# A feed-forward stage run in two halves of its inner width, with partial sums kept in DRAM

## The chip, the cores and the metric

The kernel runs on one core of one Trainium2 chip. The metric is the device time of one execution in microseconds (us). A core has five engines that work through their own queues in order: TensorE (PE, matrix products; PEld is its weight load), VectorE (DVE), ScalarE (ACT), GpSimd (POOL) and SyncE (SP, which here only starts transfers). Results of products go to PSUM, everything else lives in SBUF, and transfers to and from DRAM are started from the queues of SP, ACT and POOL.

## The reference

Three layers follow one another: a gated recurrent attention (4 x 8 heads, 768 steps, head size 40), a mixture of 8 experts of which each token takes one, and a plain feed-forward layer. Only the last is touched by the change:

```python
def _moe_ref(x, w_gate, w1, w2):            # x: 3072 tokens x 320
    ...
    out[mask] = gate_w[mask, None] * (np.maximum(xe @ w1[e], 0.0) @ w2[e])

def _moe2_ref(x, w_in, w_out):              # w_in: 320 x 2048, w_out: 2048 x 320
    h = x @ w_in
    g = np.maximum(0.01 * h, h)
    return (g @ w_out).astype(np.float32)
```

The expert's gate weight is one factor per token, and the leaky maximum is homogeneous for positive factors, so the kernel multiplies by it at the very end.

## The kernel before

Every product is made of three: each factor is split into a high part (rounded by ACT) and a low part (the rest, subtracted by DVE or GpSimd), and high x high, low x high and high x low are summed in PSUM.

After the attention, the expert stage runs over eight experts, each with a fixed share of up to 512 tokens. Expert e computes eight first-layer sums (`expert_up`, 8 inner pieces f) and then three groups of second-layer sums (`expert_down`, a = 0, 1, 2), which are copied into `x2T`, the transposed input of the feed-forward, 3072 tokens and 512 spare columns wide. For a = 2 ACT copies half of the rows (L1409) and DVE adds the other half (L1410). During expert 7's three groups `ffn_x` also splits the first 512 tokens of the feed-forward (`xf`).

The feed-forward `ffn` runs over six windows of 512 tokens and, within each, over 16 inner pieces f of 128 columns: loop index i = 0 to 95. For each i TensorE does eight products of 512 columns (`up`, L217, quarter f // 4 of `w_in`), ACT scales by 0.01 (L1540), DVE takes the maximum (L1541), ACT rounds the high part (L1544) and DVE subtracts the low part (L1546). Three pieces later (LAG) come twelve products of 320 columns (`down`, L1506 to L1508), which add into four PSUM accumulators `po`, one for each 128 tokens. They live in four banks, so the next window's sums can begin only when the last window's are evicted. At f = 15 they are evicted with the gate factor, two by DVE (L1517), two by ACT (L1515), and scattered to their rows of the result by POOL (`put_rows`, L93). The first three inner pieces' products with the first two thirds of x are issued ahead, because the last third comes late.

The feed-forward's weights come as 8-byte numbers and are converted on the chip while the experts and the feed-forward run. There are 20 pieces: `("i", quarter, a)`, 12 of them, and `("o", f2, 0)`, eight output pieces of two f each. A piece takes five steps (`piece_step`), step n belonging to piece n // 5: step 0 stores the piece before (two transfers on ACT's queue, each behind the part that it stores) and takes exponent and mantissa apart (DVE, L1247 and L1248); step 1 is one ACT operation (L1250); step 2 two on DVE (L1255, L1256); step 3 one on DVE (L1260) and ACT's rounding (L1275); step 4 two on GpSimd (L1280, L1281), and the raw load of a later piece. Scratch tiles `d_e`, `d_a`, `d_s` exist once.

`run_side` does the next step. In the experts it is called at the places listed in `SIDE` (numbers 0 to 7 are the first-layer pieces, 8 to 13 the two halves of each second-layer group), in the feed-forward after L1544 (k = 0) and after L1546 (k = 1) of each inner piece. Before the feed-forward 66 steps are done (expert 7's last group holds steps 64 and 65); it does the other 35 at 2.25 per inner piece.

The tiles of three input quarters are there all along; the fourth quarter's can be had only when the experts' hidden tiles (`hh`, `hl`) are free, so its pieces (the stored ones) are converted into scratch, written to DRAM (`wi_d`) and loaded by POOL's queue at the start of the feed-forward (L1337). The output weights lie in tiles that the experts' weights leave free (`wo_tiles`). All converted output pieces, and the fourth input quarter, are also kept in DRAM for a closing loop over tokens beyond the experts' shares, which runs zero times here.

Of the kernel before, what the change touches and what calls it, by code (L numbers as in the profile page):

```python
# [51 lines left out]
def tile_mlstm_moe_ffn(  # L52
# [24 lines left out]
    xs_d = dp.tile([E * NT, DM], F32, tag="xs_d", name="xs_d")  # L77
    list_d = dp.tile([NT, 2], I32, tag="list_d", name="list_d")
    wi_d = dp.tile([2, 3, P, CAP], F32, tag="wi_d", name="wi_d")
    wo_d = dp.tile([2, NF, P, DM], F32, tag="wo_d", name="wo_d")  # L80
    g_d = dp.tile([BH, S], F32, tag="g_d", name="g_d")

# [1141 lines left out]
    def stored(q):  # L1224

        kind, i, j = pieces[q]
        return kind == "i" and i >= NQ - 1

    def piece_step(n):
        q, t = divmod(n, 5)  # L1230
        if t == 0 and q > 0:
            piece_store(pieces[q - 1])
        if q >= len(pieces):
            return
        p = pieces[q]
        kind, i, j = p
        n = CAP if kind == "i" else 2 * DM
        raw = st["raw", p]
        coded = raw.dtype != F32

        def tmp(tg, dt=I32):
            return mp.tile([P, 2 * DM], dt, tag=tg, name=f"{tg}{kind}{i}_{j}")[:, 0:n]

        if t == 0 and coded:
            h = raw[:, :, 1]
            ex, man = st["ex"], st["man"] = tmp("d_e"), tmp("d_a")
            nc.vector.tensor_scalar(ex, h, 20, 0x7FF, ALU.logical_shift_right, ALU.bitwise_and)  # L1247
            nc.vector.tensor_scalar(man, h, 12, 9, ALU.logical_shift_left, ALU.logical_shift_right)  # L1248
        if t == 1 and coded:
            nc.scalar.activation(st["ex"], st["ex"], AF.Relu, bias=bexp, scale=2.0**23)  # L1250
        if t == 2 and q > 0 and stored(q - 1) and q + 1 < len(pieces):
            piece_load(pieces[q + 1])
        if t == 2 and coded:
            sc = st["sc"] = tmp("d_s")
            nc.vector.scalar_tensor_tensor(sc, raw[:, :, 1], -(2**31), st["ex"], ALU.bitwise_and, ALU.bitwise_or)  # L1255
            nc.vector.tensor_tensor(st["man"], st["man"], sc, ALU.bitwise_or)  # L1256
        if t == 3:
            if coded:
                w = raw[:, :, 0].bitcast(U32)
                nc.vector.scalar_tensor_tensor(st["ex"].bitcast(F32), w, 2.0**-52, st["sc"].bitcast(F32), ALU.mult, ALU.mult)  # L1260
            val = st["val"] = st["man"].bitcast(F32) if coded else raw
            if kind == "i" and i < NQ - 1:
                st["hl"] = [(wiq[i][0][j], wiq[i][1][j], slice(0, n))]
                st["out", p] = None
            elif kind == "o":
                cut = [(0, 2)] if wo_at(2 * i)[2] == wo_at(2 * i + 1)[2] else [(0, 1), (1, 2)]
                st["hl"] = st["out", p] = [
                    (wo_at(2 * i + a)[0][:, 0 : (b - a) * DM], wo_at(2 * i + a)[1][:, 0 : (b - a) * DM], slice(a * DM, b * DM)) for a, b in cut
                ]
            else:  # L1270

                lo = raw.rearrange("p n t -> p (n t)")[:, 0:n].bitcast(F32R) if coded else tmp("d_s", F32R)
                st["hl"] = st["out", p] = [(tmp("d_h", F32R), lo, slice(0, n))]
            for hi, _, sl in st["hl"]:
                nc.scalar.copy(hi, val[:, sl])  # L1275
        if t == 4:
            for hi, lo, sl in st["hl"]:
                val = st["val"][:, sl]
                if coded:
                    nc.gpsimd.tensor_tensor(val, val, hi.bitcast(F32), ALU.subtract)  # L1280
                    nc.gpsimd.tensor_tensor(lo, val, st["ex"].bitcast(F32)[:, sl], ALU.add)  # L1281
                else:
                    nc.gpsimd.tensor_tensor(lo, val, hi.bitcast(F32), ALU.subtract)
            st.pop(("raw", p))
            if q + 2 < len(pieces) and not stored(q):
                piece_load(pieces[q + 2])
# [13 lines left out]
    wo_t = {}  # L1300

    def wo_tiles(nm, part):
        if part == 0:
# [10 lines left out]
        i, r = (0, f) if f < 8 else (1, f - 8) if f < 14 else (0, 8) if f == 14 else (2, 0)  # L1314
        return wo_t[i, 0][:, r * DM :], wo_t[i, 1][:, r * DM :], (i, f == 14)

    pieces = [("i", qd, a) for qd in range(NQ) for a in range(3)] + [("o", f2, 0) for f2 in range(NF // 2)]
    side_at = [0]

    def run_side(end=5 * len(pieces)):  # L1320
# [4 lines left out]
    def load_wo(f0, f1):  # L1325
        for hl in range(2):
            nc.gpsimd.dma_start(
                wo_at(f0)[hl][:, 0 : (f1 - f0) * DM].rearrange("p (a d) -> p a d", d=DM), wo_d[hl, f0:f1].rearrange("a p d -> p a d")
            )

    def load_wi(nm):
        ih = [t[0] for t in wiq]
        il = [t[1] for t in wiq]
        for hl, (dl, tg) in enumerate(((ih, "hh"), (il, "hl"))):
            ts = [mp.tile([P, CAP], F32R, tag=tg, name=f"wi{nm}{tg}{a}", bufs=8) for a in range(3)]
            for a in range(3):
                nc.gpsimd.dma_start(ts[a], wi_d[hl, a])  # L1337
            dl.append(ts)
        return ih, il

    def tiles_fx(nm, odd=0):
        return tiles_x(f"f{nm}", "xr", "raw") if odd else tiles_x(f"f{nm}")
# [83 lines left out]
    for i in range(24):  # L1426
        extras.setdefault((2 + i // 4, 2 * (i % 4) + 1), []).append(lambda i=i: list_rows(i, i + 1))
    SA = 5, 6, 7, 8, 9, 11, 13
    SB = 0, 1, 4, 6, 7, 9, 11, 13
    SC = 0, 1, 4, 6, 7, 9, 11, 13  # L1430
    SD = 0, 1, 4, 6, 7, 9, 11, 13
    SE_ = 0, 1, 4, 6, 7, 9, 11, 13
    SF = 0, 1, 4, 6, 7, 9, 11, 13
    SG = 0, 1, 4, 6, 7, 9, 11, 13
    SH = 0, 1, 4, 6, 7, 8, 9, 10, 11, 12, 13

    SIDE = (SA, SB, SC, SD, SE_, SF, SG, SH)

# [4 lines left out]
    for e in range(E):  # L1443
# [11 lines left out]
        if not last:  # L1455
            e_r = nc.sync.value_load(slots[0:1, 0, e + 1 : e + 2], min_val=0, max_val=E - 1)
            row = nc.sync.value_load(slots[0:1, 1, e + 1 : e + 2], min_val=0, max_val=(E - 1) * NT)
            xr = x_rows_tile(e + 1)
            x_load(xr, row, 0, CAPS[e + 1])
            w1raw = load_w1(of_expert(w1, e_r), e + 1)  # L1460
            w1n = tiles_w1(e + 1)
            xs = tiles_x(e + 1)
        else:
            xf = tiles_fx("a0")
            assert side_at[0] <= 5 * 3 * NQ + 3
            wo_tiles("a", 0)
        w2u = w2s

        def in_down(a, k, e=e, last=last):
# [17 lines left out]
            w1s = w1n  # L1487
            w2raw, w2s = load_w2(of_expert(w2, e_r), e + 1), tiles_w2(e + 1)

    def ffn(nm, wins, wi, metas, x0, side=lambda i, k: None, W=CAP):  # L1490
        wih, wil = wi
        nw = len(wins)
        xs = {0: x0}
        gs, pos = {}, {}
        LAG = 3

        def down(fs, w):
            if fs[0] == 0:
                pos[w] = [pm.tile([P, DM], F32, tag="dn" if n < 2 else "tr", name=f"po{nm}{w}_{n}") for n in range(W // P)]
            po = pos[w]  # L1500
            gw = [gs.pop(w * NF + f) for f in fs]
            for n in range(W // P):
                tsl = slice(n * P, (n + 1) * P)
                for f, (g_h, g_l) in zip(fs, gw):
                    woh, wol = (t[:, 0:DM] for t in wo_at(f)[0:2])
                    nc.tensor.matmul(po[n], g_h[:, tsl], woh, start=(f == 0), stop=False)  # L1506
                    nc.tensor.matmul(po[n], g_h[:, tsl], wol, start=False, stop=False)  # L1507
                    nc.tensor.matmul(po[n], g_l[:, tsl], woh, start=False, stop=(f == NF - 1))  # L1508
                if fs[-1] < NF - 1:
                    continue  # L1510
                mt = metas(w, n)
                ot = mp.tile([P, DM], F32, tag=("d_e", "d_s", "d_a", "d_h")[n], name=f"ot{nm}{w}_{n}")
                gate = mt[:, 1:2].bitcast(F32)
                if n % 2:
                    nc.scalar.activation(ot, po[n], AF.Copy, scale=gate)  # L1515
                else:
                    nc.vector.tensor_scalar(ot, po[n], gate, None, ALU.mult)  # L1517
                put_rows(out_w, (), out, mt[:, 0:1], ot)

        FIRST = 4  # L1520
        pus = {}

        def up(i, part):
            w, f = divmod(i, NF)
# [3 lines left out]
            up_mms(pus[i], xs[w], wih[f // 4], wil[f // 4], fs, part)  # L1528

        for i in range(FIRST - 1):  # L1530
            up(i, slice(0, 6))
        for i in range(nw * NF + LAG):
            if i < nw * NF:
                w, f = divmod(i, NF)
# [11 lines left out]
                nc.vector.tensor_tensor(g_l, lk, g_h.bitcast(F32), ALU.subtract)  # L1546
                side(i, 1)
                gs[i] = g_h, g_l
                if f == 10 and w + 1 < nw:
                    xs[w + 1] = ffn_x(tiles_fx(f"{nm}{w + 1}", (w + 1) % 2), wins[w + 1])  # L1550
            if i >= LAG:
                w, f = divmod(i - LAG, NF)
                if w + 1 < nw or f < NF - 4:
                    down([f], w)
                elif f == NF - 3:
                    down([NF - 4], w)
                elif f == NF - 1:
                    down([NF - 3, NF - 2, NF - 1], w)
# [12 lines left out]


    n_win = nc.values_load(tab[0:1, 0, 0:1], min_val=0, max_val=MW)
# [75 lines left out]
```

## Time and profile before

| | us |
|---|---|
| median of 3 timed runs | 779.99 |
| lowest and highest | 776.85, 780.35 |
| the profiled execution, whole | 781.25 |
| its span | 779.5 |
| its TensorE busy | 733.8 (94%) |
| its DVE busy | 469.3 (60%) |
| its ACT busy | 364.5 (47%) |
| its GpSimd busy | 256.5 (33%) |

The profile is of one execution. The span is the time from its first to its last instruction; the whole time has 1.75 us around it. Rows of it are shown below in groups: a row of the timeline has start and duration in us, then engine, line of the kernel, operation, output <- inputs, sizes; in square brackets the idle time of the engine just before and what ended it. A busy time of TensorE is modelled, so stretches in which it is busy throughout but at half its clock also count as busy; the granted clock stands beside it.

### The profile page before, as it was taken

How to read it: one execution, taken by the hardware profiler on the slowest of the kernel's cores; microseconds unless marked ns; L12 is line 12 of the kernel's file. 1: busy time of each engine (PE TensorE's matmuls, PEld its weight loads, DVE VectorE, ACT ScalarE, POOL GpSimd, SP SyncE). 2: the span in 40 equal slices, each digit the busy share in tenths (PEclk: the TensorE clock that was granted, in tenths of full speed). 3: DMA queues.
4: the chain of work that ended last, by engine and by line, in shares of the span. 5: the costliest groups of instructions: out<-in, count | busy, mean ns of one | idle time of the engine just before them, and what ended most of it. 6: DMA issues, size and time to landing. Idle time of an engine off the chain costs nothing.

```text
span 779.5 us, 12185 instructions
## 1 busy us (share of the span) xinstructions
PE 733.8 (94%) x4226; PEld 646.7 (83%) x4226; DVE 469.3 (60%) x1023; ACT 364.5 (47%) x799; POOL 256.5 (33%) x414
## 2 busy tenths in 40 slices
PE   8998999988989999999899979999999999999992
PEld 4786877877868899999897768999999999998992
DVE  6576777875687766778576776544344344344330
ACT  4675765523445545656444444343333343343330
POOL 7645667517133344246444333101002002002002
PEclk7998999987999999999999999999999999999996
DMA  6899566233635656765867421000000000000001
GB/s 165 253 321 298 162 179 198 92 99 111 187 111 179 166 131 175 165 150 143 228 131 235 144 90 60 26 1 18 18 1 26 9 1 34 1 1 34 1 1 37
DMA packets 58320, 85.31 MB, mean 109 GB/s; under 512 B 9423, under 2 KB 38895, under 8 KB 58255
## 3 DMA queue, kind: packets, MB, share of 16 engines
q1 hardware_dynamic: 44975, 56.67, 26.4%
q10 hardware_dynamic: 9344, 18.35, 7.5%
q0 software_dynamic: 3936, 9.47, 3.6%
q8 instruction: 35, 0.57, 0.3%
q14 instruction: 30, 0.25, 0.1%
HBM read 64.42 MB, written 19.95 MB: 108 GB/s over the span
## 4 chain that ended last, share of the span: by engine, by line
issue 35%; PE 19%; DVE 7%; POOL 6%; DMA 5%; ACT 3%; ACTq 0%; POOLq 0%; SPq 0%; DVEq 0%
PE pu L217 9%; PE pd L1403 8%; POOL out_dram L93 3%; DMA w1r<-in_moe_w_dram 3%; POOL d_ao L1280 1%; PE pt L243 1%; DVE lka L1541 1%; POOL woaw1l L1281 1%; DVE d_ao L1256 1%; DVE d_so L1255 1%; ACT d_eo L1250 1%; PE pva L217 1%; DVE w1l L164 1%; DMA rdo<-in_moe_w_out_dram 1%; DVE hl L248 1%
## 5 line engine op out<-in xcount | busy, mean ns | idle before, releaser
L217 PE MATMUL pva<-xhfa,wi 128*128 128x512 f32 x432 | 134.2, 393 | 0.0
L1541 DVE TENSOR_TENSOR lka<-pva,lka 128x512 f32<-128x512 f32 x96 | 66.3, 691 | 108.2 <-ACT lka L1540 106.3
L1540 ACT ACTIVATE lka<-pva 128x512 f32<-128x512 f32 x96 | 57.2, 596 | 120.1 <-PE pva L217 110.2
L93 POOL DMA_INDIRECT out_dram<-ota,meta x24 | 24.0, 999 | 263.8 <-DVE ota L1517 259.7
L1546 DVE TENSOR_TENSOR gla<-lka,gha 128x512 fp32r<-128x512 f32 x96 | 67.9, 707 | 59.0 <-ACT gha L1544 58.3
L1544 ACT CAST gha<-lka 128x512 fp32r<-128x512 f32 x96 | 59.6, 621 | 84.2 <-DVE lka L1541 81.2
L217 PEld LDWEIGHTS pva<-xhfa,wi 128*128 128x128 f32 x432 | 78.4, 188 | 12.7 <-DVE xhfa L198 0.2
L1508 PE MATMUL poa<-woaw1h,gla 128*128 128x320 f32 x216 | 67.1, 310 | 2.0 <-DVE gla L1546 2.0
L546 ACT ACTIVATE E<-pD,wn 128x128 f32<-128x128 f32 x192 | 56.1, 366 | 25.5 <-PE pD L543 19.7
L217 PE MATMUL pu<-xh,w1h 128*128 128x256 f32 (+7 forms) x192 | 65.8, 344 | 1.8 <-DVE xh L198 1.7
L1506 PE MATMUL poa<-woaw1h,gha 128*128 128x320 f32 x216 | 66.7, 309 | 0.7 <-ACT ota L1515 0.7
L1507 PE MATMUL poa<-woaw1l,gha 128*128 128x320 f32 x216 | 66.8, 309 | 0.1
L217 PE MATMUL pu<-xh,w1l 128*128 128x256 f32 (+7 forms) x192 | 65.2, 341 | 0.0
L589 PEld LDWEIGHTS pI<-nv,P 128*128 128x128 f32 x384 | 54.2, 202 | 10.3 <-DVE P L557 4.7
L589 PE MATMUL pI<-nv,P 128*128 128x123 f32 (+1 forms) x384 | 56.6, 284 | 3.4 <-DVE P L557 3.4
L217 PE MATMUL pva<-xlfa,wi 128*128 128x512 f32 x144 | 56.0, 389 | 0.0
L555 PE MATMUL pS<-qB,nK 120*128 120x384 f32 (+1 forms) x132 | 54.9, 498 | 0.0
L1507 PE MATMUL poa<-woaw2l,gha 128*128 128x320 f32 x144 | 45.9, 319 | 5.1 <-POOL woaw2l L1281 5.1
L1403 PE MATMUL pd<-hh,w2h 128*128 128x512 f32 (+6 forms) x128 | 46.0, 359 | 0.0
L1508 PE MATMUL poa<-woaw2h,gla 128*128 128x320 f32 x144 | 45.8, 318 | 0.1
L1506 PE MATMUL poa<-woaw2h,gha 128*128 128x320 f32 x144 | 45.5, 316 | 0.4 <-ACT gha L1544 0.2
L1403 PE MATMUL pd<-hl,w2h 128*128 128x512 f32 (+6 forms) x128 | 45.6, 356 | 0.2 <-DVE hl L248 0.2
(302 smaller groups left out, 1825.6 us busy)
## 6 DMA issues: line engine op xcount, KB each, us to landing
w2r<-in_moe_w_dram SPq DMA_DIRECT2D x16, 640.0 KB
w1r<-in_moe_w_dram SPq DMA_DIRECT2D x16, 512.0 KB
xs_d<-zr SPq DMA_DIRECT2D x16, 320.0 KB
rdo<-in_moe_w_out_dram ACTq DMA_DIRECT2D x16, 320.0 KB
w1r<-in_moe_w_dram SPq DMA_DIRECT2D x32, 128.0 KB
rdi<-in_moe_w_in_dram ACTq DMA_DIRECT2D x8, 512.0 KB
no<-in_o_gate_dram SPq DMA_DIRECT2D x12, 320.0 KB
nv<-in_v_dram SPq DMA_DIRECT2D x10, 328.0 KB
```

Of the source, the lines that this page charges most:

```text
L217: nc.tensor.matmul(ps_t, a, b, start=start, stop=stop)
L546: nc.scalar.activation(Et[:, j], pD[:, j], AF.Exp, bias=wn[:, c, 3, HG * g + j : HG * g + j + 1])
L555: nc.tensor.matmul(pS[:, :nh], nats["K", c][:R, g], QB[p][:R, g - GCUT[p], :nh], start=True, stop=True)
L589: nc.tensor.matmul(pI[:, r0:, j], Pt[:, j], vj, start=True, stop=True)
L1403: nc.tensor.matmul(pd, aa, bb, start=(i == 0), stop=(i == len(seq) - 1))
L1506: nc.tensor.matmul(po[n], g_h[:, tsl], woh, start=(f == 0), stop=False)
L1507: nc.tensor.matmul(po[n], g_h[:, tsl], wol, start=False, stop=False)
L1508: nc.tensor.matmul(po[n], g_l[:, tsl], woh, start=False, stop=(f == NF - 1))
L1540: nc.scalar.activation(lk, pu, AF.Copy, scale=0.01)
L1541: nc.vector.tensor_tensor(lk, pu, lk, ALU.max)
L1544: nc.scalar.copy(g_h, lk)
L1546: nc.vector.tensor_tensor(g_l, lk, g_h.bitcast(F32), ALU.subtract)
```

## The change

The feed-forward's loop order becomes: half h of the inner width (8 of the 16 inner pieces), and within it all six windows. Each of the 12 units (h, w) has its own sums, and each window's tokens are split into high and low parts twice. At the end of a unit of the first half the four accumulators are evicted with the gate factor (two by DVE, two by ACT as before), three of them into the spare columns of `x2T`, and stored to DRAM (`part_d`) by SP's queue. In the second half the stored sums are loaded at the beginning of the unit (SP's queue, tile tag `rawd`), and DVE evicts all four accumulators with one operation that multiplies by the gate and adds the stored part; the result is scattered as before.

The order of the pieces becomes: nine input pieces, output pieces 0 to 3, the last input quarter, output pieces 4 to 7. Output pieces 0 and 1 are now the ones that are converted into scratch, stored and loaded again (`load_wo(0, 4)`, POOL's queue, behind the stores); the last input quarter is converted in place, in `hh` and `hl` tiles, during the first half. Together with output pieces 4 to 7 that makes seven pieces whose conversion lies wholly in the first half. The experts 1 to 6 do seven steps each instead of eight, expert 7 thirteen instead of eleven, the feed-forward one per inner piece: 62 steps are done before it, expert 7's last group holds steps 60 and 61, and the last step is at inner piece 38.

```diff
+    part_d = dp.tile([NT // CAP, P, CAP // P, DM], F32, tag="part_d", name="part_d")
...
     def stored(q):
 
         kind, i, j = pieces[q]
-        return kind == "i" and i >= NQ - 1
+        return kind == "o" and i < NPRE
...
-            elif kind == "o":
+            elif kind == "i":
+                st["hl"] = st["out", p] = [(wi3[0][j], wi3[1][j], slice(0, n))]
+            elif i >= NPRE:
...
+    NPRE = 2
...
-    pieces = [("i", qd, a) for qd in range(NQ) for a in range(3)] + [("o", f2, 0) for f2 in range(NF // 2)]
+    pieces = [("i", qd, a) for qd in range(NQ - 1) for a in range(3)] + [("o", f2, 0) for f2 in range(NF // 4)]
+    pieces += [("i", NQ - 1, a) for a in range(3)] + [("o", f2, 0) for f2 in range(NF // 4, NF // 2)]
...
-    SB = 0, 1, 4, 6, 7, 9, 11, 13
...
-    SH = 0, 1, 4, 6, 7, 8, 9, 10, 11, 12, 13
+    SB = 0, 1, 4, 6, 9, 11, 13
+    SC = SD = SE_ = SF = SG = SB
+    SH = 0, 1, 3, 4, 5, 6, 7, 8, 9, 10, 11, 12, 13
...
             xf = tiles_fx("a0")
...
             wo_tiles("a", 0)
+            load_wo(0, 2 * NPRE)
...
+        nf = NF // parts
+        units = [(h, w) for h in range(parts) for w in range(len(wins))]
...
+        def down(fs, u):
+            h, w = units[u]
+            f0, f1 = h * nf, h * nf + nf - 1
+            if fs[0] == f0:
+                pos[u] = [pm.tile([P, DM], F32, tag="dn" if n < 2 else "tr", name=f"po{nm}{u}_{n}") for n in range(W // P)]
+                if h > 0:
+                    before[u] = wp.tile([P, W // P, DM], F32, tag="rawd", name=f"pb{nm}{u}", bufs=2)
+                    nc.sync.dma_start(before[u], part_d[w])
...
+                if h + 1 < parts and n < 3:
+
+                    ot = x2T[:, n, NT : NT + DM]
+                else:
+                    ot = mp.tile([P, DM], F32, tag="d_h" if h + 1 < parts else ("d_e", "d_s", "d_a", "d_h")[n], name=f"ot{nm}{u}_{n}")
+                if h > 0:
+                    nc.vector.scalar_tensor_tensor(ot, po[n], gate, before[u][:, n], ALU.mult, ALU.add)
+                elif n % 2:
                     nc.scalar.activation(ot, po[n], AF.Copy, scale=gate)
                 else:
                     nc.vector.tensor_scalar(ot, po[n], gate, None, ALU.mult)
-                put_rows(out_w, (), out, mt[:, 0:1], ot)
+                if h + 1 < parts:
+                    nc.sync.dma_start(part_d[w, :, n], ot)
+                else:
+                    put_rows(out_w, (), out, mt[:, 0:1], ot)
...
-                if f == 10 and w + 1 < nw:
-                    xs[w + 1] = ffn_x(tiles_fx(f"{nm}{w + 1}", (w + 1) % 2), wins[w + 1])
+                if i % nf == nf // 2 + 2 - parts and u + 1 < len(units):
+                    xs[u + 1] = ffn_x(tiles_fx(f"{nm}{u + 1}", (u + 1) % 2), wins[units[u + 1][1]])
...
     def ffn_side(i, k):
-        for _ in range(1 + (k == 1 and i % 4 == 3)):
+        if k == 0:
             run_side()
         if (i, k) == (4, 1):
             load_meta()
-        if (i, k) == (20, 1):
+        if (i, k) == (44, 1):
             windows()
 
-    ffn("a", list(range(NT // CAP)), load_wi("a"), lambda w, n: meta[:, 4 * w + n], xf, ffn_side)
+    ffn("a", list(range(NT // CAP)), tiles_wi("a"), lambda w, n: meta[:, 4 * w + n], xf, ffn_side, parts=2)
```

## Rows read from the trace of the kernel before

**Rows 1.** Table by stretches: bounds, length, busy us (instructions) by engine, clock, DMA share, GB/s.

```profile
404.32:484.41 80.09, 71.58 (x358) 61.38 (x357) 55.57 (x81) 36.33 (x61) 31.23 (x25) 0.96 0.45 142
...
598.94:656.43 57.49, 57.49 (x322) 52.11 (x321) 24.96 (x38) 21.89 (x37) 4.38 (x8) 1.00 0.04 12
```

**Rows 2.** Timeline of TensorE: the feed-forward's first product and its last.

```profile
404.32 0.62 PE L217 MATMUL pva<-xhfa,wi 128*128 128x512 f32 x2
...
764.02 0.31 PE L1508 MATMUL poa<-woaw2m,gla 128*128 128x320 f32 x1
```

**Rows 3.** TensorE's waits, 395 to 480 and (last) 480 to 780: total, times, longest.

```profile
PE poa L1507 <- POOL woaw2l L1281: 5.1, 3, 2.9
PE poa L1508 <- DVE gla L1546: 2.0, 2, 1.1
...
PE poa L1506 <- ACT ota L1515: 0.7, 1, 0.7
```

**Rows 4.** Table by stretches, at three stretches of the lower clock.

```profile
381.30:384.70 3.40, 3.40 (x13) 3.40 (x12) 2.71 (x3) 1.54 (x4) 3.03 (x2) 0.51 0.83 212
446.20:449.60 3.40, 3.40 (x13) 3.21 (x13) 2.68 (x5) 2.11 (x4) 0.00 (x0) 0.50 0.69 254
466.70:470.10 3.40, 3.29 (x12) 3.29 (x13) 2.92 (x5) 1.93 (x3) 0.06 (x1) 0.50 0.30 98
```

**Rows 5.** Timeline of GpSimd, DVE and TensorE at the end of a converted output piece.

```profile
465.22 1.53 POOL L1281 TENSOR_TENSOR woaw2l<-d_ao,d_eo 128x640 fp32r<-128x640 f32 x1
466.79 0.49 DVE L1247 TENSOR_SCALAR d_eo<-rdo 128x640 int32<-128x640 int32 x1 [2.09 <-POOL woaw2l L1281]
466.81 0.64 PE L1507 MATMUL poa<-woaw2l,gha 128*128 128x320 f32 x1 [2.87 <-POOL woaw2l L1281]
```

**Rows 6.** Timeline of DVE and ACT at the end of the second window.

```profile
540.01 0.69 DVE L1546 TENSOR_TENSOR gla<-lka,gha 128x512 fp32r<-128x512 f32 x1 [0.69 <-ACT gha L1544]
540.62 1.00 DVE L1517 TENSOR_SCALAR ota<-poa,meta 128x320 f32<-128x320 f32 x2
...
541.60 0.60 ACT L1540 ACTIVATE lka<-pva 128x512 f32<-128x512 f32 x1 [0.77 <-PE pva L217]
```

**Rows 7.** Groups by line, 404 to 484: count, busy us, mean ns; idle before.

```profile
L1280 POOL TENSOR_TENSOR d_ao<-d_ao,woaw1h 128x640 f32<-128x640 f32 (+1 forms) x5 | 8.8, 1761 | 23.1 <-ACT woaw1h L1275 18.6 <-DVE gla L1546 4.5
...
L1256 DVE TENSOR_TENSOR d_ao<-d_ao,d_so 128x640 int32<-128x640 int32 x7 | 5.8, 826 | 0.2
```

**Rows 8.** Groups by line, 490 to 764.

```profile
L196 ACT CAST xhfa<-x2T 128x512 fp32r<-128x512 f32 (+1 forms) x12 | 6.6, 617 | 0.0
...
L198 DVE TENSOR_TENSOR xlfa<-x2T,xhfa 128x512 fp32r<-128x512 f32 x8 | 5.2, 685 | 0.0
```

**Rows 9.** Timeline of DVE, ACT and GpSimd, from expert 7's end into the feed-forward.

```profile
397.67 0.48 DVE L248 SCALAR_TENSOR_TENSOR hl<-pu,hh 128x320 fp32r<-128x320 f32 x1
...
407.24 1.10 DVE L198 TENSOR_TENSOR xhfa<-x2T,xhfa 64x512 fp32r<-64x512 f32 x1 [0.69 <-ACT xhfa L196]
...
399.65 0.43 ACT L1406 COPY x2T<-pd 128x320 f32 x1 [4.12 <-POOL gap L92]
...
409.17 0.60 ACT L1540 ACTIVATE lka<-pva 128x512 f32<-128x512 f32 x1 [1.96 <-PE pva L217]
...
406.23 1.56 POOL L1281 TENSOR_TENSOR woaw1l<-d_ao,d_eo 128x640 fp32r<-128x640 f32 x1
407.74 1.78 POOL L1337 DMA_DIRECT2D wiahh<-wi_d  x3
```

**Rows 10.** The chain of waits through 366 to 382, its longest piece.

```profile
368.48 9.38 DMA w1r<-in_moe_w_dram
```

**Rows 11.** Timeline of ACT's queue and of TensorE at the change to expert 7.

```profile
367.83 0.44 ACTq L1293 DMA_DIRECT2D wi_d<-rdi  x1
...
380.23 0.64 PE L243 MATMUL pt<-ident,xr 128*128 128x128 f32 x3 [2.31 <-DVE xl L198]
```

**Rows 12.** Table by stretches, at the start of the feed-forward.

```profile
404.00:412.00 8.00, 8.00 (x38) 6.52 (x37) 4.69 (x8) 3.12 (x6) 6.93 (x8) 1.00 1.09 295
```

More of the change, by code (lines that the diff above doesn't have):

```diff
@@ L1298, in piece_store @@
                     )
-    wo_t = {}
+    NPRE = 2
+    wo_t, wi3 = {}, []
     def wo_tiles(nm, part):
@@ L1329, in load_wo, with tiles_wi @@
             )
+    def tiles_wi(nm):
+        wi3[:] = [[mp.tile([P, CAP], F32R, tag=tg, name=f"wi{nm}{tg}{a}", bufs=8) for a in range(3)] for tg in ("hh", "hl")]
+        return [[t[hl] for t in wiq] + [wi3[hl]] for hl in range(2)]
     def load_wi(nm):
[L1332 to L1335, printed above, removed]
+        wi = tiles_wi(nm)
+        for hl in range(2):
             for a in range(3):
-                nc.gpsimd.dma_start(ts[a], wi_d[hl, a])
-            dl.append(ts)
-        return ih, il
+                nc.gpsimd.dma_start(wi3[hl][a], wi_d[hl, a])
+        return wi
     def tiles_fx(nm, odd=0):
@@ L1428, in tile_mlstm_moe_ffn @@
     SA = 5, 6, 7, 8, 9, 11, 13
-    SB = 0, 1, 4, 6, 7, 9, 11, 13
[L1430 to L1434, printed above, removed]
-    SH = 0, 1, 4, 6, 7, 8, 9, 10, 11, 12, 13
+    SB = 0, 1, 4, 6, 9, 11, 13
+    SC = SD = SE_ = SF = SG = SB
+    SH = 0, 1, 3, 4, 5, 6, 7, 8, 9, 10, 11, 12, 13
     SIDE = (SA, SB, SC, SD, SE_, SF, SG, SH)
@@ L1464, in tile_mlstm_moe_ffn @@
             xf = tiles_fx("a0")
-            assert side_at[0] <= 5 * 3 * NQ + 3
+            assert 1 <= side_at[0] - 5 * (3 * (NQ - 1) + NPRE) <= 3
             wo_tiles("a", 0)
+            load_wo(0, 2 * NPRE)
         w2u = w2s
@@ L1488, in tile_mlstm_moe_ffn, with ffn, place @@
             w2raw, w2s = load_w2(of_expert(w2, e_r), e + 1), tiles_w2(e + 1)
-    def ffn(nm, wins, wi, metas, x0, side=lambda i, k: None, W=CAP):
+    def ffn(nm, wins, wi, metas, x0, side=lambda i, k: None, W=CAP, parts=1):
         wih, wil = wi
-        nw = len(wins)
+        nf = NF // parts
+        units = [(h, w) for h in range(parts) for w in range(len(wins))]
         xs = {0: x0}
-        gs, pos = {}, {}
+        gs, pos, before = {}, {}, {}
         LAG = 3
[L1497 to L1501, printed above, removed]
+        def place(i):
+            u, f = divmod(i, nf)
+            return u, units[u][0] * nf + f
+        def down(fs, u):
[6 more added lines that the diff above has]
+                    nc.sync.dma_start(before[u], part_d[w])
+            po = pos[u]
+            gw = [gs.pop(u * nf + f - f0) for f in fs]
             for n in range(W // P):
@@ L1505, in down @@
                     woh, wol = (t[:, 0:DM] for t in wo_at(f)[0:2])
-                    nc.tensor.matmul(po[n], g_h[:, tsl], woh, start=(f == 0), stop=False)
+                    nc.tensor.matmul(po[n], g_h[:, tsl], woh, start=(f == f0), stop=False)
                     nc.tensor.matmul(po[n], g_h[:, tsl], wol, start=False, stop=False)
-                    nc.tensor.matmul(po[n], g_l[:, tsl], woh, start=False, stop=(f == NF - 1))
-                if fs[-1] < NF - 1:
+                    nc.tensor.matmul(po[n], g_l[:, tsl], woh, start=False, stop=(f == f1))
+                if fs[-1] < f1:
                     continue
                 mt = metas(w, n)
-                ot = mp.tile([P, DM], F32, tag=("d_e", "d_s", "d_a", "d_h")[n], name=f"ot{nm}{w}_{n}")
                 gate = mt[:, 1:2].bitcast(F32)
-                if n % 2:
+                if h + 1 < parts and n < 3:
[5 more added lines that the diff above has]
+                elif n % 2:
                     nc.scalar.activation(ot, po[n], AF.Copy, scale=gate)
@@ L1523, in up @@
         def up(i, part):
-            w, f = divmod(i, NF)
+            u, f = place(i)
             if i not in pus:
@@ L1527, in up @@
             fs = slice((f % 4) * P, (f % 4 + 1) * P)
-            up_mms(pus[i], xs[w], wih[f // 4], wil[f // 4], fs, part)
+            up_mms(pus[i], xs[u], wih[f // 4], wil[f // 4], fs, part)
         for i in range(FIRST - 1):
             up(i, slice(0, 6))
-        for i in range(nw * NF + LAG):
-            if i < nw * NF:
-                w, f = divmod(i, NF)
+        total = len(units) * nf
+        for i in range(total + LAG):
+            if i < total:
+                u, f = place(i)
                 if i == FIRST - 2:
@@ L1548, in ffn @@
                 gs[i] = g_h, g_l
-                if f == 10 and w + 1 < nw:
-                    xs[w + 1] = ffn_x(tiles_fx(f"{nm}{w + 1}", (w + 1) % 2), wins[w + 1])
+                if i % nf == nf // 2 + 2 - parts and u + 1 < len(units):
+                    xs[u + 1] = ffn_x(tiles_fx(f"{nm}{u + 1}", (u + 1) % 2), wins[units[u + 1][1]])
             if i >= LAG:
-                w, f = divmod(i - LAG, NF)
-                if w + 1 < nw or f < NF - 4:
-                    down([f], w)
+                u, f = place(i - LAG)
+                if u + 1 < len(units) or f < NF - 4:
+                    down([f], u)
                 elif f == NF - 3:
-                    down([NF - 4], w)
+                    down([NF - 4], u)
                 elif f == NF - 1:
-                    down([NF - 3, NF - 2, NF - 1], w)
+                    down([NF - 3, NF - 2, NF - 1], u)
     wo_tiles("a", 1)
     def ffn_side(i, k):
-        for _ in range(1 + (k == 1 and i % 4 == 3)):
+        if k == 0:
             run_side()
```

## The prediction, made before the changed kernel ran

> **What bounds the kernel now.** The page's engine totals come first: TensorE is the busiest engine by far, so time comes off only where it stands still or runs slowly. Where in the feed-forward it does, the table by stretches shows, cut at the first result scatter of each token window: a full window of sixteen inner pieces takes 57.49 us, and TensorE is busy for all of it at clock 1.00, DVE for 24.96, ACT for 21.89 [rows 1]. One inner piece (eight 512-column products, twelve 320-column ones) therefore costs 57.49 / 16 = 3.593 us, and 96 of them 344.9. From the first feed-forward product at 404.32 to the end of the last (764.02, and about 0.15 before another could follow) lie 359.85 us [rows 2]. The feed-forward loses 14.9 us, and the stretch to the first scatter (404.32 to 484.41), with 8.5 us of idle TensorE and clock 0.96 [rows 1], holds nearly all of it. The list of waits names who ends the idle time: 5.1 us GpSimd's lower parts of the output weights (L1281), 2.0 us DVE's lower parts of the activations (L1546), 0.7 us the eviction at the end of the first window [rows 3]. Twice the granted clock is at 0.50 for 3.4 us, the lower of its two levels (1.2 instead of 2.4 GHz), right behind such waits [rows 4], which costs 1.7 each. That is 7.8 + 3.4 = 11.2; the other 3.7 is slow refilling after each wait and waits of under 0.3 us.
>
> The mechanism shows at 463 to 467: GpSimd finishes the lower part of a weight piece at 466.75, DVE has waited 2.09 us for it (the next piece reuses the scratch tiles), and TensorE 2.87 [rows 5]. Into the first window 35 steps of conversion are pressed, 2.25 per inner piece, and each output piece is done just ahead of its first use.
>
> **The change, part by part.**
>
> *Conversion thinned out (removes).* One step per inner piece instead of 2.25. Steps 62 to 100 fall on inner pieces 0 to 38 of 96. Before the stage eleven pieces are done, not twelve. Output pieces 0 to 3 serve the first half; the last input quarter (steps 65 to 79, pieces 3 to 17) and output pieces 4 to 7 (steps 80 to 99, to piece 37) are first wanted in the second half, at piece 48. So no weight is converted just ahead of its use any more, except pieces 2 and 3 at the start. DVE's load per inner piece: 0.69 twice for the activations [rows 6], and one fifth of a conversion, (0.49 x 2 + 0.82 x 3) / 5 = 0.7 (0.49 in rows 5, 0.826 in rows 7), so 2.1 of 3.59. GpSimd's two operations (1.76 and 1.53 us [rows 5, 7]) fit into the nearly two inner pieces between the steps that bracket them. This takes away the 14.9 us; what is late next follows.
>
> *The start of the stage (moves).* Here the new phase of the steps matters. The queues of ACT, DVE and GpSimd run in order. In expert 7's last product group the steps now are 60 and 61, where they were 64 and 65. Step 60 opens a new piece: ACT must issue the store of output piece 2, and waits for GpSimd's lower part of it; DVE waits for the same. It stands ahead of the copy of L1409, the add of L1410 and the last split of window 0's tokens, without which no first-layer sum can close. How such a store blocks ACT shows in expert 7 already: its copy at 399.65 came after 4.12 us of waiting [rows 9]. When is GpSimd done? Before, the corresponding piece ended at 406.23 + 1.56 = 407.79 [rows 9]. Now it comes one slot earlier, but the steps in expert 7's up phase are denser (seven, not five), and two reloads of output weights stand ahead on GpSimd (about 0.6 us each, from 1.78 for three [rows 9]), which wait for the store of output piece 1. I estimate 408.4. Then the store's issue (0.44 in rows 11), the copy and the add (0.43 and 0.48 for the like ones in rows 9), ACT's split 0.62 and DVE's 0.69 [rows 8], 0.1 for hand-overs: 411.2, where the split was done at 407.24 + 1.10 = 408.34 [rows 9]. That is 2.9 us late; step 62 (DVE, 2 x 0.82) then lies ahead of the first L1546, about 0.5 more. Start: 3.4 us. Bounds: 0, if GpSimd ends two microseconds earlier, and 6.5, if the reloads wait about the 4.12 us of rows 9.
>
> *Clock.* Of the four waits of about 1.1 us in the first window (two on L1546 with 2.0 in all, and 5.1 - 2.9 = 2.2 in two on L1281 [rows 3]) one was followed by a low stretch, and so was the one of 2.87 [rows 4, 5]. The start holds two waits of that size; I take half of one stretch, 0.85; bounds 0 and 3.4.
>
> *Reload of four output pieces' worth of rows (adds), quarter of input weights no longer reloaded (removes).* 1.31 MB instead of 1.57 MB through GpSimd's queue, wanted for the first second-layer product at about 414.4 (411.2 and 14 first-layer products at 0.23 us, their share by columns of 3.593). Nothing, as long as it lands by then; see the second rival.
>
> *Twice as many ends of sums.* There are 11 hand-overs of the four accumulators instead of 5. A steady one costs nothing: DVE ends L1546 at 540.70, evicts two (1.00 us), ACT the other two, and TensorE computes first-layer sums until 541.60 [rows 6]. In the first half six evict as before, with one conversion step in between; only at piece 10 does the long step (1.65 us) fall in front, which ends the first eviction at about 542.2 instead of 541.6: 0.6. Bounds 0 and 6 x 0.7 [rows 3]. In the second half DVE does all four, with an add of the stored half. No such operation is in the trace; the nearest are L248 (PSUM and SBUF, 320 columns, 0.48 [rows 9]) and L1517 (1.00 for two [rows 6]). Four end at 540.70 + 4 x 0.5 = 542.7; TensorE wants the fourth at 541.60 + 3 x 0.44 = 542.9. I take 0.3 for the five, bounds 0 and 5 x 0.7.
>
> *Splitting each window twice.* Six more splits: three ACT copies (about 0.62) and three DVE subtractions (0.69 [rows 8]) per eight inner pieces, four pieces (14 us) ahead of their use. Covered by idle ACT and DVE; without that cover some 2 us each.
>
> *Partial sums.* 24 stores of 160 KB and six loads of 640 KB on SP's queue, which has nothing else there; DMA share in a steady window is 0.04 [rows 1], and the load is issued eight inner pieces (29 us) ahead. Nothing. The end is the same order of products, with DVE's eviction for ACT's: nothing.
>
> *Experts.* Seven steps each instead of eight. At the change to expert 7 TensorE waited 2.31 us for a token split that stood behind w1's load (9.38 us) [rows 10, 11], and a low stretch followed [rows 4]. The store of the last input quarter's piece, issued at 367.83 [rows 11], shared the DMA engines with that load; it is gone from there, and of the step that stood between, DVE's two operations become one on ACT. I take 0.7 gained; bounds 0.5 lost and 4.0 gained.
>
> **Sum.** After: 3.4 + 0.85 + 0.6 + 0.3 = 5.15 lost in the stage instead of 14.9, so 9.75 gained, with the experts 10.4. The profiled execution took 781.25 us (span 779.5), 1.26 over the median of 779.99 and above all three timed runs. 781.25 - 10.4 = 770.9; on the median's scale 769.6.
>
> **The rivals.**
>
> *The start is covered.* GpSimd is done in time, no low stretch: loss 0.9 to 1.5, gain 13.4 to 14, with 0.7 from the experts 14.4: 765.6. For it: before, ACT waited for TensorE at 409.17 and not the other way round [rows 9]. Against: ACT's order in the code. Chance 0.17.
>
> *The start jams.* Reload or store late: 6.5, two low stretches 3.4, hand-overs 0.9, together 10.8; gain 4.1 + 0.7 = 4.8: 775.2. For it: from 404 to 412 the DMA engines are full (share 1.09, 295 GB/s [rows 12]). Reload, raw pieces and store come to about 3.1 MB there, which at that rate takes 10.6 us from 404.5, to 415, when it is wanted at 414.4. Chance 0.17. The Trainium skill, "DMA: Bandwidth & Descriptors", section "Issuing engines are not separate DMA queues", says that transfers from different issuing engines interleave on the same 16 DMA engines. By that rule the reload gains nothing from having GpSimd's queue to itself; the full share in rows 12 agrees, and the time would be this rival's.
>
> *Every hand-over stops TensorE (slower).* Place: the first second-layer product after each of 11 ends. If evictions fall behind by 1 us and the clock falls each time (1.7), 11 x 2.7 = 29.7 + 4.25 is lost instead of 14.9, 0.7 from the experts off: 798. It decides from (14.9 + 0.7 - 4.25) / 11 = 1.03 us per hand-over. Against: the steady ones lose nothing at clock 1.00 [rows 1, 6]. Chance 0.05. The Trainium skill, "TensorE: Matmul & The Clock Gate", section on HAM oscillation, tells of a kernel whose clock fell before every tile because of a wait there; no row here shows that at a hand-over.
>
> *It does not do what it says.* The waits stay, because DVE and GpSimd collide in any spacing (L1281 ran 1.53 to 1.56 us and DVE waited behind it [rows 5, 9]): 780. Chance 0.04.
>
> **How the numbers follow.** The forecast keeps 0.57. The range, 763.5 to 776.5, takes in the first two rivals but their outer ends, and the bounds of the start. A measurement tells 0.5% (3.9 us) from no change, so faster means under 776.1: forecast 0.57, first rival 0.17, half of the second 0.08, together 0.82; same 0.12; slower 0.06.
>
> **What would show it.** Right: in the stretch table no TensorE idle from about 420 on, clock 1.00 to the end, first-half units of 28.7 us; ACT waiting for GpSimd's L1281 right ahead of L1409; first L1540 at 411 to 412. Wrong: waits of poa on ota at each eighth inner piece; a wait of the first second-layer product for the reload's DMA; more than one low stretch behind 404.

## The result and the profile after

The changed kernel took 768.58 us (median of 4 runs, 766.67 to 772.99) beside 778.68 for the kernel before (776.85 to 780.35): a ratio of 0.9889, 95% interval 0.9858 to 0.992. Forecast were 769.6 and a range of 763.5 to 776.5. The profiled execution is the slowest of the four, 772.99 us; its span is 771.3.

The total came out as forecast; its parts did not. The table by stretches of the changed kernel, cut at the first feed-forward product (409.38), shows both sides (bounds, length, busy us and instructions of PE, PEld, DVE, ACT and POOL, clock, DMA share, GB/s):

```profile
364.00:384.00 20.00, 15.42 (x79) 14.17 (x78) 10.65 (x20) 7.53 (x17) 3.63 (x3) 0.83 0.69 145
384.00:409.38 25.38, 21.48 (x134) 20.96 (x133) 18.98 (x31) 11.89 (x26) 15.28 (x16) 0.93 0.59 150
409.38:425.00 15.62, 14.47 (x72) 12.01 (x71) 10.32 (x16) 6.43 (x12) 4.68 (x3) 1.00 0.61 159
425.00:580.00 155.00, 155.00 (x864) 140.27 (x863) 103.25 (x175) 75.42 (x131) 22.05 (x18) 1.00 0.22 74
580.00:756.40 176.40, 176.40 (x990) 159.76 (x988) 88.15 (x138) 67.67 (x114) 25.45 (x45) 1.00 0.14 47
```

From 425 to the end TensorE stands still nowhere and its clock is 1.00; between 409.38 and 425 it stands still for 1.15 us. Before, it lost 8.5 us of idle time in the first window alone [rows 1]. But the first feed-forward product comes at 409.38, five us later than before [rows 2], and the 45 us ahead of it have 8.5 us of idle TensorE and clocks of 0.83 and 0.93. The list of TensorE's waits from 360 to 425 (who waited for whom, total, times, longest) names them:

```profile
PE pt L244 <- DVE xl L199: 4.6, 1, 4.6
PE pd L1410 <- DVE w2l L187: 3.9, 2, 3.4
PE poa L1524 <- DVE gla L1572: 0.6, 1, 0.6
PE pva L218 <- DVE xhfa L199: 0.6, 1, 0.6
```

The first two lie in the experts: the token split at the change to expert 7 (2.31 us before [rows 11]), and a new one, the split of expert 7's second weights. In the first the clock falls to its lower level, 1.2 GHz, while TensorE still waits (the wait ends at 379.36); in the second it falls as the wait ends:

```profile
377.20:384.00 6.80, 4.64 (x15) 4.19 (x16) 5.59 (x8) 4.25 (x10) 2.67 (x2) 0.50 0.41 111
401.10:404.50 3.40, 3.29 (x12) 3.29 (x13) 1.93 (x6) 1.76 (x3) 2.67 (x3) 0.50 0.57 104
```

One table holds the traces of this case by stage. The stages run from the start to expert 0's first product, from there to the first feed-forward product, from there to the end of the last (its start and 0.15 us), and from there to the end of the span; all in us, each from one profiled execution.

| kernel | attention | experts | feed-forward | end | span |
|---|---|---|---|---|---|
| before | 193.8 | 210.5 | 359.9 | 15.3 | 779.5 |
| changed | 191.2 | 218.2 | 347.1 | 14.9 | 771.3 |
| e1 changed, again | 191.8 | 216.4 | 346.4 | 14.1 | 768.7 |
| e2 eight steps per expert | 188.7 | 210.0 | 347.2 | 14.7 | 760.5 |
| e3 halves alone | 191.6 | 210.1 | 363.1 | 15.0 | 779.9 |
| e4 dense conversion | 189.5 | 215.7 | 364.2 | 14.1 | 783.5 |
| e5 no steps in the last group | 189.7 | 216.0 | 345.4 | 14.6 | 765.7 |
| e6 one step shifted | 189.9 | 213.6 | 346.8 | 14.2 | 764.5 |
| e7 1.5 steps per piece | 189.3 | 215.6 | 354.3 | 13.9 | 773.1 |
| e8 e2 and one step moved | 192.0 | 208.9 | 347.4 | 14.3 | 762.6 |
| e9 no partial sums | 190.9 | 212.3 | 346.2 | 14.3 | 763.7 |
| e10 e8 and e5 together | 191.3 | 208.8 | 346.3 | 14.5 | 760.9 |

96 inner pieces at 3.593 us are 344.9; what the feed-forward column has above that is lost. The attention's code is the same in all of them, and its time differs by 5 us.

### The profile page after: what moved, and what is told of

It is laid out like the page before. It is cut to its first block, busy times and chain, and to the rows that moved or that the text cites. A ratio compares the mean times of both kernels' runs of the same rounds, so it can differ in the third digit from the quotient of the medians.

```text
span 771.3 us, 12337 instructions
## 1 busy us (share of the span) xinstructions
PE 725.5 (94%) x4226; PEld 640.9 (83%) x4226; DVE 491.2 (64%) x1065; ACT 372.6 (48%) x817; POOL 255.1 (33%) x410
## 5 line engine op out<-in xcount | busy, mean ns | idle before, releaser
L1572 DVE TENSOR_TENSOR gla<-lka,gha 128x512 fp32r<-128x512 f32 x96 | 70.1, 730 | 50.5 <-ACT gha L1570 49.4
L218 PEld LDWEIGHTS pva<-xhfa,wi 128*128 128x128 f32 x432 | 78.2, 188 | 13.4 <-DVE xhfa L199 1.0
L590 PEld LDWEIGHTS pI<-nv,P 128*128 128x128 f32 x384 | 53.8, 200 | 10.4 <-DVE P L558 4.9
L1410 PE MATMUL pd<-hh,w2l 128*128 128x512 f32 (+6 forms) x128 | 46.3, 362 | 3.9 <-DVE w2l L187 3.9
L165 POOL TENSOR_TENSOR w1l<-w1r,w1h 128x512 fp32r<-128x512 f32 x14 | 19.9, 1424 | 82.0 <-ACT w1h L164 82.0
L248 ACT ACTIVATE hh<-pu 128x256 fp32r<-128x256 f32 (+7 forms) x64 | 31.7, 501 | 29.7 <-PE pu L218 26.9
```

What stands on the lines that cost most here:

```text
L218: nc.tensor.matmul(ps_t, a, b, start=start, stop=stop)
L590: nc.tensor.matmul(pI[:, r0:, j], Pt[:, j], vj, start=True, stop=True)
L1410: nc.tensor.matmul(pd, aa, bb, start=(i == 0), stop=(i == len(seq) - 1))
```

## The experiments

Times are medians; the ratio is to runs of the kernel before on the same chip (777.43 for e1 to e4, 778.39 for e5 to e8, 777.55 for e9 and e10).

**e1: the changed kernel again.** No edit.

> The changed kernel once more, for a second trace. In its first trace the feed-forward lost 2.1 us instead of 14.9 (gain 12.8), but the stretch before it, from expert 6's last groups to the first feed-forward product, lost about 8 us (a 4.9 us step ahead of the transposes of L244, 3.4 us on L187, and 10 us at the lower clock). Theory A (the loss in the experts comes from the change's order of steps): both waits come again within 1 us, and the time is 767 to 770. Theory B (the loss belonged to that one execution, whose load of w1 was slow): the wait at L244 is 2 to 3 us as before the change, only that on L187 comes again, 766 to 768.

770.23 us, ratio 0.9895 (0.981 to 0.998). TensorE's waits from 360 to 425:

```profile
PE pd L1410 <- DVE w2l L187: 3.9, 2, 3.4
PE pt L244 <- DVE xl L199: 2.3, 1, 2.3
PE poa L1524 <- DVE gla L1572: 0.6, 1, 0.6
```

The wait on L187 came again to the tenth. It belongs to the change: all seven traces with the changed kernel's steps in expert 7's first layer have a wait of 3.2 to 3.4 us there (changed, e1, e4 to e7, e9), and none of the five without them has one. The one on L199 is back at its old 2.3, so the extra 2.3 us of the first trace were that execution's. The waits are as theory B said; the time lies above both ranges. Experts 5.9 us longer than before, feed-forward 13.4 shorter.

**e2: the experts' old rate.**

```diff
-    SB = 0, 1, 4, 6, 9, 11, 13
+    SB = 0, 1, 4, 6, 7, 9, 11, 13
-    SH = 0, 1, 3, 4, 5, 6, 7, 8, 9, 10, 11, 12, 13
+    SH = 0, 1, 4, 8, 9, 10, 11, 12, 13
```

> The changed kernel with the old rate of conversion in the experts: eight steps each for experts 1 to 6, and three instead of seven in expert 7's first layer. Theory A (seven steps within expert 7's first layer block ACT and DVE behind GpSimd and delay the split of w2, L187): the wait of L1410 on L187 (3.4 us) and the low clock behind it (1.7) go, 3 to 5 us faster than the changed kernel, about 764 to 765. Rival (the delay only moves into expert 6, which now gets the store of output piece 0): no more than 1 us either way, 768.

762.70 us, ratio 0.9822 (0.9744 to 0.99). The waits of the same stretch:

```profile
PE pt L244 <- DVE xl L199: 2.4, 1, 2.4
PE poa L1524 <- DVE gla L1572: 0.5, 1, 0.5
```

L187 is gone from the list, and the experts take 210.0 us again. Theory A holds, and the gain is larger than forecast, 5.9 us against the first runs and 7.5 against e1. The new wait comes from the seven steps in expert 7's first layer. But e2 takes away two things at once: four of these steps, and with them GpSimd's two operations of output piece 1, which in the changed kernel fall between the splits of w2. It also does 64 steps ahead of the feed-forward instead of 62, and one hand-over there waits 0.4 us.

**e3: the loop order alone.** The kernel before with the new `ffn`, `parts=2` and `part_d`; pieces, stores, reload and rates as before.

> The kernel before with only the loop order of the feed-forward changed: two halves, partial sums in DRAM, but pieces in their old order, the last input quarter stored and reloaded, 2.25 steps per inner piece. Theory A (deadlines: a wait costs only where a weight is wanted soon): output pieces 0 to 3 are still just in time, so the waits up to inner piece 8 stay (about 3.5 us of the old 14.9) and those behind vanish; no loss in the experts; 11 us faster than before, 768. Rival (density: 2.25 steps per inner piece make DVE and GpSimd late wherever the weights are wanted): waits on L1546 and low clock stay through inner piece 15, gain 3 to 5 us, 774 to 776.

781.88 us, ratio 1.0054 (1.0024 to 1.0084): slower, against both theories. Timeline of TensorE (the end of unit 0 and the next second-layer product) and of DVE:

```profile
441.15 0.31 PE L1520 MATMUL poa<-woaw1h,gla 128*128 128x320 f32 x1
452.57 0.61 PE L1518 MATMUL poa<-woaw1h,gha 128*128 128x320 f32 x1 [9.27 <-DVE x2T L1535]
...
451.88 1.00 DVE L1535 TENSOR_SCALAR x2T<-poa,meta 128x320 f32<-128x320 f32 x2
```

The sums of unit 0 were complete at about 441.5, and DVE evicted them at 451.88. The eviction stands in DVE's queue behind the activations of the three inner pieces by which TensorE runs ahead, with their conversion steps. The clock falls to its lower level in this wait and stays there for 10.2 us, in 5.13 of which TensorE works:

```profile
447.50:457.70 10.20, 5.13 (x17) 4.77 (x18) 8.39 (x14) 5.38 (x10) 3.10 (x2) 0.50 0.60 210
```

The kernel before has no hand-over until the end of its first window; here one comes after half of it, and it calls DVE's arrears in at once.

**e4: the changed kernel with the old rate.**

```diff
-        if k == 0:
+        for _ in range(1 + (k == 1 and i % 4 == 3)):
             run_side()
```

> The changed kernel with 2.25 steps per inner piece as before, so that the conversion is over at inner piece 17 instead of 38, though nothing of it is wanted before piece 48. Theory A (deadlines): the feed-forward loses at most 2 us more than in the changed kernel (waits on L1546 of about 1 us, two before the change), 768 to 771. Rival (density): the feed-forward loses 8 us or more again, 776 to 780.

785.84 us, ratio 1.0096 (1.0055 to 1.0136). But for the last three steps of output piece 3 (62 to 64), nothing of what is converted there is wanted before inner piece 48, and still the feed-forward loses 19.3 us. TensorE's waits from 425 on:

```profile
PE poa L1522 <- ACT ota L1537: 9.4, 1, 9.4
PE poa L1522 <- ACT gha L1570: 1.8, 2, 1.2
PE poa L1522 <- ACT x2T L1537: 1.7, 1, 1.7
```

Theory A, that a wait costs only where a weight is wanted soon, is out, and the time is above the rival's range too. It is the rate, and most of it strikes at the first hand-over. The last 2.57 us ahead of ACT's two evictions were not its own work:

```profile
452.42 1.93 POOL L1284 TENSOR_TENSOR woaw2l<-d_ao,d_eo 128x640 fp32r<-128x640 f32 x1
454.38 0.38 ACTq L1299 DMA_DIRECT2D wo_d<-woaw2l  x1
454.80 0.53 ACT L1537 ACTIVATE x2T<-poa,meta 128x320 f32<-128x320 f32 x1 [2.57 <-DMA rdo<-in_moe_w_out_dram]
```

The row names a load, but the evictions stand in ACT's queue behind the store of output piece 4's low part, which was issued as GpSimd ended that part at 454.35. DVE's two evictions came only at 455.19, also behind a wait for that part (1.42 us). So the arrears are not busy time alone: at steps that open the next piece the queues also stand still behind GpSimd, DVE for 5.5 us between 425 and 456.

**e5: no steps ahead of the last copy.**

```diff
-    SH = 0, 1, 3, 4, 5, 6, 7, 8, 9, 10, 11, 12, 13
+    SH = 0, 1, 3, 4, 5, 6, 7, 8, 9, 10, 11
```

> The changed kernel without steps 60 and 61 in expert 7's last product group; they run with inner pieces 0 and 1, and the conversion ends at piece 40. Theory A (step 60 holds ACT and DVE behind GpSimd ahead of the copy of L1416, as the prediction's step on the start said): ACT's wait of 3.1 us ahead of that copy goes, and with it the two waits of 0.6 us of TensorE behind it; the feed-forward loses under 1 us instead of 1.5 to 2.1; at most 2 us faster in all, 767 to 769. Rival (the copy is late for the products of group 2 themselves): the waits stay as they are.

766.81 us, ratio 0.9824 (0.9759 to 0.9889). ACT's copy of L1416, first in the changed kernel, then in e5, from the two timelines:

```profile
410.94 0.38 ACTq L1299 DMA_DIRECT2D wo_d<-woaw1l  x1
411.37 0.42 ACT L1416 COPY dsm<-pd 64x320 f32<-64x320 f32 x1 [3.06 <-POOL woaw1l L1284]
```

```profile
405.95 0.42 ACT L1416 COPY dsm<-pd 64x320 f32<-64x320 f32 x1 [1.27 <-PE pd L1410]
```

ACT now waits for TensorE's product and no longer for GpSimd; TensorE's two waits of 0.6 are gone, and the feed-forward takes 345.4, 0.5 above what its products need. Theory A holds. The total moved by less than the runs scatter (764.24 to 768.61 beside 766.67 to 772.99).

**e6: one step later.** `SH = 0, 2, 3, ...` instead of `0, 1, 3, ...`.

> The changed kernel with one step of expert 7 moved by one first-layer piece: step 50, which stores output piece 0, follows piece 2 instead of piece 1. Theory A (ACT and DVE are blocked behind GpSimd's low part of output piece 0 for 2.5 us, and that delay arrives at the split of w2): ACT's wait ahead of L248 falls by 1.2 us or more and TensorE's 3.4 us on L187 by as much or to nothing; 1 to 4 us faster, about 766 to 769. Rival (DVE is late by its own work and by collisions with GpSimd, two operations of 1.65 and 1.89 us instead of 0.29 and 0.69): the wait on L187 stays at 2.5 us or more.

767.55 us, ratio 0.9854 (0.9789 to 0.9919). ACT's wait ahead of L248 fell from 2.52 to 0.65, TensorE's wait stayed:

```profile
PE pd L1410 <- DVE w2l L187: 3.2, 1, 3.2
```

The rival holds: what delays the split is not the block at the store. DVE's timeline in the changed kernel, and GpSimd's beside it, show the rest:

```profile
391.87 0.29 DVE L189 TENSOR_TENSOR w2m<-w2r,w2m 128x128 fp32r<-128x128 f32 x1
...
395.96 0.68 DVE L187 TENSOR_TENSOR w2l<-w2r,w2h 128x512 fp32r<-128x512 f32 x1
396.56 1.65 DVE L189 TENSOR_TENSOR w2m<-w2r,w2m 128x128 fp32r<-128x128 f32 x1
398.13 0.81 DVE L1261 SCALAR_TENSOR_TENSOR d_eo<-rdo,d_so 128x640 f32<-128x640 uint32 x1
...
399.27 1.89 DVE L187 TENSOR_TENSOR w2l<-w2r,w2h 128x512 fp32r<-128x512 f32 x1
...
396.49 1.57 POOL L1283 TENSOR_TENSOR d_ao<-d_ao,d_ho 128x640 f32<-128x640 f32 x1 [2.45 <-ACT d_ho L1278]
399.08 1.53 POOL L1284 TENSOR_TENSOR rdo<-d_ao,d_eo 128x640 fp32r<-128x640 f32 x1 [1.01 <-issue]
```

The same operations take 0.29 and 0.68 us when GpSimd has no such operation. By these rows 2.6 us of the 3.4 go to the overlap with GpSimd's two operations, and 0.8 is the step's own time at 398.13, which in the kernel before stood behind the last split. That division is an estimate; no run separates the two.

**e7: a rate between.** `if k == 0 or i % 2 == 1`, 1.5 steps per inner piece.

> The changed kernel with 1.5 steps per inner piece in the feed-forward, between its 1 and the 2.25 of the kernel before. Theory A (a threshold: DVE and ACT fall behind only where the chain of one inner piece with its steps takes longer than TensorE's 3.59 us; at 2.25 it takes about 4.1 to 4.2, at 1 under 3.59): at 1.5 the chain stays at or under 3.6, the lower parts come 3 to 7 us behind the products, no hand-over waits over 1 us, and the time is that of the changed kernel within 2 us, 768 to 771. Rival (the loss grows with the rate all the way): a hand-over wait of 2 to 5 us and a third to half of the 15 us of the dense kernel, 773 to 777.

774.83 us, ratio 0.9966 (0.9933 to 0.9999). One wait from 425 on (it ends at 446.74), and again a low stretch that begins in it:

```profile
PE poa L1522 <- ACT x2T L1537: 4.1, 1, 4.1
445.50:452.30 6.80, 5.42 (x16) 4.66 (x17) 4.81 (x9) 3.09 (x6) 1.87 (x2) 0.50 0.48 160
```

The feed-forward takes 347.1 us at 1 step per inner piece, 354.3 at 1.5 and 364.2 at 2.25. In this trace the lower parts (L1572) of inner pieces 0 to 10 ended 3.4 us apart on average (413.48 to 447.53), less than TensorE's 3.59, and the wait came all the same: there is no free rate up to 3.59 us of chain, and the loss grows with the rate, as the rival said. The extra steps of e4 and e7 stand behind the lower part (k = 1), and each rate puts other steps beside the first hand-over; neither was varied by itself.

**e8: one step less beside the token split.** e2 with `SG = 0, 1, 4, 6, 7, 11, 13` and `SH = 0, 1, 4, 6, 8, ...`.

> The kernel of e2_side8 with the long conversion step moved away from the first token split of expert 7 (expert 6 leaves out its step there, expert 7 does one more). Theory A (the wait of L244 on L199, 2.4 us, and the low clock behind it come from w1's late load and from DVE's two operations of that step, 2.5 us): the wait falls to 1 us or less and the low stretch may go; 1 to 3 us faster than e2_side8, about 760 to 762. Rival (the load of w1 alone sets it): unchanged within 1 us, 762 to 763.

763.89 us, ratio 0.9798 (0.9733 to 0.9863). From the list of TensorE's waits from 190 to 425:

```profile
PE pt L244 <- DVE xl L199: 1.4, 2, 0.8
PE pt L244 <- DMA xr<-xs_d: 1.4, 1, 1.4
PE pd L1410 <- DVE hl L249: 0.9, 1, 0.9
```

The longest wait on the split fell from 2.4 to 0.8 and no stretch of the experts or the feed-forward is at the lower clock. But a wait for the tokens' load and one on L249 stand in its place; with 1.1 us less in the experts the time cannot be told from e2 and lies above both ranges.

**e9: no partial sums.** Stores and loads of `part_d` and the add left out, evictions by DVE and ACT in turn in both halves; the result is then the second half's sums alone.

> The changed kernel with the stores, the loads and the add of the partial sums left out, and evictions shared by DVE and ACT in both halves; the first half's sums are dropped, so the result is the second half's alone. Theory A (the transfers and DVE's four evictions lie beside TensorE's work): the same as the changed kernel within 1 us, 767 to 770. Rival (they cost something at the hand-overs or at the start, through the DMA engines): 2 to 4 us faster, 764 to 766.

766.32 us, ratio 0.9857 (0.9803 to 0.9912). The feed-forward takes 346.2 beside 347.1 and 346.4 with them. The partial sums' traffic and DVE's four evictions cost nothing that can be seen there. The total lies between the two ranges, and what the trace is shorter by lies in the experts (no long wait at L199 in it), not where the sums are.

**e10: e8 with e5's edit.**

> The kernel of e8_side8b without steps in expert 7's last product group, as in e5_nolast. Theory A (the waits at the start of the feed-forward and in the experts add up): the feed-forward loses under 1 us instead of 2.2 to 2.5, no low clock between the experts' start and the end; 760 to 763, 15 us below the kernel before. Rival (what is saved at the start is waited for elsewhere): 763 to 765.

762.04 us, ratio 0.9808 (0.977 to 0.9846). All its six runs (759.25 to 765.62) lie below all eight of the changed kernel (765.85 to 775.24), so it is faster than the changed kernel and than the one before. It does not beat e2 and e8 by anything measurable. The feed-forward loses 1.4 us, not under 1, with this left in the list from 190 to 425:

```profile
PE poa L1525 <- DVE gla L1573: 0.6, 1, 0.6
```

## Why the forecast held, step by step

The total held; of the two stages that the change touches, one gained more than forecast and the other lost where a gain was forecast.

*The feed-forward's loss of 14.9 us goes.* Right, and by more than forecast: 2.1 and 1.5 us are left in two traces, where 5.15 were expected; 12.8 and 13.4 gained instead of 9.75. The reason given was double: fewer steps per inner piece, and no weight wanted soon. The second alone is not enough: with the deadlines moved but the rate kept (e4) no wait on a late weight is left in the list, and the loss was 19.3; with the loop order alone (e3) it was 18.2. The thinning alone, in the old loop order, was not run, since there the weights are wanted within the first window. The halves serve only by making room for the thinning: alone they put a hand-over into the time in which DVE and ACT are most in arrears. (The prediction counts eleven pieces done ahead of the stage instead of twelve; by steps, 62 and 66, they are twelve instead of thirteen. Its sum does not use the count.)

*The start, 3.4 us.* The mechanism was right. GpSimd ended its part at 410.92, step 60's store was issued at 410.94, ACT's copy came after 3.06 us of idle time, and taking the step away removed that wait (e5). The size was too large. The sum put GpSimd's end 4.1 us behind the first feed-forward product (408.4 against 404.32); it came 1.5 behind it, and in e1 with it (408.17 and 408.19), because the experts' loss had made the first product itself 5.1 and 3.9 us later than before. So the last split of window 0's tokens ended 4.8 us after the first product, where it was 4.0 before: 0.8 late, not 2.9, and in e1 (3.2 after it) not late at all.

```profile
413.47 0.69 DVE L199 TENSOR_TENSOR xhfa<-x2T,xhfa 64x512 fp32r<-64x512 f32 x1 [0.69 <-ACT xhfa L197]
```

TensorE lost 0.6 us by it in the first trace and nothing in e1. Step 62's two operations ahead of the first lower part cost the other 0.6, in both traces, where 0.5 was forecast. e5 gained 1.0 to 1.7 in the stage.

*The clock, 0.85.* There is no low stretch in the feed-forward of either trace; the waits were 0.6, not 1. The low stretches came before it.

*Hand-overs, 0.9.* Nothing: no wait of TensorE from 425 on. DVE's new operation took 0.546 us, beside 0.5 assumed from the nearest rows [rows 6, 9]:

```profile
L1535 DVE SCALAR_TENSOR_TENSOR ota<-poa,meta,pba 128x320 f32<-128x320 f32 x24 | 11.8, 546 | 2.8 <-PE poa L1524 2.8
599.00:627.74 28.74, 28.74 (x162) 25.93 (x161) 14.65 (x24) 11.27 (x20) 4.61 (x8) 1.00 0.14 46
```

The second row is a whole unit of the second half: 28.74 us, 8 x 3.593, as in the window before [rows 1]. The rival of a stop at each hand-over did not come about in the changed kernel. Its mechanism exists: in e3, e4 and e7 one hand-over did hold TensorE, for 9.3, 9.4 and 4.1 us, and the clock fell in each of these waits.

*Reload, partial sums, second splitting.* Free, as said: TensorE has no wait for a reload in the lists, and none at all from 425 on; e9 shows it for the sums by themselves.

*The experts, 0.7 gained.* Wrong: 7.7 lost in one trace, 5.9 in the other, 210.5 us against 218.2 and 216.4, outside the bounds of 0.5 lost and 4.0 gained. The seven traces with these steps in expert 7's first layer have experts of 212.3 to 218.2 us, the five without 208.8 to 210.5. The step that failed counted the seven steps of expert 7's first layer only as a later end for GpSimd (0.6 us). What was missed is that three of them (50, 52 and 53) also lie on DVE ahead of splits of w2 in its queue, where before two did, and that the GpSimd part of step 54 lengthens those splits: 3.4 us of TensorE's time and 1.7 or more at the lower clock beside it, in both traces. The text asks at the start of the feed-forward which queues a step passes, but not for these seven steps and DVE. The Trainium skill, "SBUF — State Buffer", section "Who interferes with whom", says that a DVE instruction with two SBUF inputs contends with a GpSimd instruction that reads SBUF. The trace agrees: 1.65 and 1.89 us instead of 0.29 and 0.68.

*The sum.* 9.75 + 0.7 = 10.4 was forecast; 12.8 - 7.7 = 5.1 came of the two stages in the first trace, with 3.0 from the attention and the end, which the change doesn't touch, and 13.4 - 5.9 = 7.5 with 3.3 in the second. That the medians differ by 10.1 is two errors of opposite sign and the scatter of the rest, so in part luck, not a sum that was right.

## What to carry to other kernels

In this kernel, work squeezed between a pipeline's own operations was limited by how far its engines may fall behind, and not only by when its result is wanted: thin it out first, and look where the next hand-over of accumulators calls the arrears in. A loop reordering can be worth only what it makes room for: here it lost time by itself (e3). When side work is taken out of one stage and pressed into another, price it there on every queue that it is put into, and at the length that operations have while two engines collide.

## What was not expected of the hardware

The stage that no edit touches, the attention, took 188.7 to 193.8 us in twelve traces, a scatter half as large as the effect. A DVE operation on 128 x 128 numbers took 1.65 us beside a GpSimd subtraction, five to six times its own length. And the clock fell inside a single wait of 9.27 us of TensorE (e3): of the 10.2 us at the lower level, 5.1 lay in the wait and 5.13 behind it with TensorE at work, so that the wait's price was about 12, the 9.3 and half of the 5.13.
